# Linear attention into a feed-forward layer: where the block sums of unit 3 and unit 4 stand in the queues

## The chip, the cores and the metric

The kernel runs on one core of a Trainium2 chip. The metric is the device time of one execution in microseconds (us), the median of several runs. Engines are named as in the profile: PE is the matmul engine (TensorE), PEld its weight load, DVE is VectorE, ACT is ScalarE, POOL is GpSimd, and SP (SPq) is the queue from which nearly all DMAs are issued. Each of them takes its instructions strictly in the order in which the program has them, and each waits at an instruction until what that needs is there.

## The reference

For every batch and head a 48 x 48 state is carried along 768 tokens, and the result goes through a feed-forward layer with SiLU.

```
B, H, S, D = 4, 8, 768, 48
for t in range(S):
    kt, vt, rt, wt = k[:, :, t], v[:, :, t], r[:, :, t], w[:, :, t]
    cur = einsum('bhd,bhe->bhde', u * kt, vt)
    y[:, :, t] = einsum('bhd,bhde->bhe', rt, state + cur)
    state = wt[..., None] * state + einsum('bhd,bhe->bhde', kt, vt)
x = y.transpose(0, 2, 1, 3).reshape(B * S, H * D)        # 3072 x 384
h = x @ w_in                                              # 384 x 2048
out = (h * sigmoid(h)) @ w_out                            # 2048 x 384
```

## The kernel before

**Units and passes.** The 768 tokens are cut into 6 chunks of 128, the 4 batches into 2 pairs: 12 units of work (`units`), each with 2 batches and 8 heads. Three stages work on a unit: the attention part (called mix), the first feed-forward matmul with SiLU (`up`, 8 steps), and the second one (`quarter`, 7 steps, a scheme with 7 block products in place of 8; the sums L967 of `sums` prepare its left factors). From unit 3 on, a loop makes one *pass* per unit: pass i holds the attention of unit i, the `up` steps of unit i-1 and the `quarter` steps of unit i-2. The attention of units 0 to 2, and all rounding of the weights, is written out by hand ahead of that loop.

**The order is written by hand.** `mix(i)` returns 13 groups of calls. The loop issues a group, then `ROOM` many of the feed-forward steps, and so on. What is called first stands first in its engine's queue. The scheduler moves nothing; it only adds the semaphore waits.

**A pass of attention.** Group 0 and 1 turn (transpose on DVE, L360) the raw w, k and r of the unit; groups 0 to 2 make running products of w on POOL (`product`, L408) and grow queries and keys by them (L608 on DVE, L626 and L635 on POOL). Levels 3 to 6 are score matmuls on PE (`burst`, L670: levels 3 and 4 together, then 5 and 6), whose outputs are kept in `score` under a mask by DVE (`keep_level`, L680). Levels 5 and 6 use the PSUM rooms p_sc and p_m. `turn_k` (L782, PE) transposes the keys into the two p_m rooms, which level 6 has to leave first. Then `y_state`, `y`, `update` (state: L827 on POOL, L836 on DVE) and `move_x`.

**The blocks of 8 tokens.** Inside a block of 8 tokens the scores aren't matmuls. `block_bonus(i, 0..7)` makes products of r, k, w and u on POOL (L488), `block_sum(i, 0..4)` reduces them on DVE (L522) into `block_sums`, `block_move` sends these through DRAM into another layout, and then `load_rk` fetches the tokens of the next unit. `block_spread` (ACT L549, L551, DVE L552) and `block_write` (DVE L558) put the result into `score`. Step 1 of `block_bonus` multiplies by `u_bc`. Its rows are loaded a second time, in the layout that units from 3 on need, by `load_u` (L259) in unit 2. `make_block_mask` is needed once, in pass 3. From pass 4 on the first products (steps 0 to 3) of unit i+1 are made at the end of pass i, and so are its first two sums and steps 4 and 5, all ahead of the next unit's turns. Pass 3 (`early` is false there, in spite of its name the test is i > 3) makes all steps of its own unit itself.

**Rooms that tie the passes.** `spare` holds three SiLU results of unit 1 until `quarter` of pass 3 has read them, and afterwards the block products (`room_b`), the sums, the moved diagonal and the mask. `quarter` writes into one of two PSUM rooms `p_o`; DVE (L994) or, for the first one, ACT (L992) empties them, so the fourth quarter can't start before DVE has added the second. In DVE's queue that addition stands behind the turns and one L608.

**SP.** The raw loads of unit i+2 (48 small DMAs, L109), the values, `move_x` (L858), the outputs (L998) and the block moves stand in one queue; most issues take about half a microsecond.

Of the kernel before, what the change touches and what calls it, by code (L numbers as in the profile page):

```python
# [8 lines left out]
F32 = mybir.dt.float32  # L9
# [29 lines left out]
def kernel(  # L39
# [11 lines left out]
    nc = tc.nc  # L51
# [4 lines left out]
    NL = 7  # L56
# [12 lines left out]
    NPAIR = 3  # L69
    FIRST = 3  # L70
    BLK = 1 << FIRST


    const = ctx.enter_context(tc.tile_pool(name="const", bufs=1))
# [95 lines left out]
    spare = const.tile([128, NSPARE * 2 * TU], F32, name="spare")  # L170
# [278 lines left out]
    R_AT, K_AT = 0, H * 2 * D  # L449
    room_b = spare[:, 0:768]  # L450
    at = 768
    block_sums = spare[:, at:at + BLK * 2 * BLK]
    at += BLK * 2 * BLK
    block_diag = [spare[:, at + b * H * BLK:at + (b + 1) * H * BLK] for b in range(NB)]
    at += NB * H * BLK
    block_both = spare[:, at:at + NB * H * BLK].rearrange("p (b h s) -> p b h s", b=NB, h=H)
# [11 lines left out]
        return bass.AP(tensor=t.tensor, offset=t.offset + start, ap=[t.ap[0], *dims])  # L468

    def at_sums(start, *dims):  # L470
        t = block_sums
        return bass.AP(tensor=t.tensor, offset=t.offset + start, ap=[t.ap[0], *dims])

    def make_block_mask():

        ids = spare[:, 0:2 * NB].rearrange("p (x b) -> p x b", x=2)
        index = room_b[:, 2 * NB:2 * NB + L].rearrange("p (i s) -> p i s", s=BLK)
        nc.gpsimd.memset(block_sums, 0.0)
        nc.gpsimd.iota(index, pattern=[[BLK, L // BLK], [0, BLK]], base=0, channel_multiplier=0,
                       allow_small_or_imprecise_dtypes=True)  # L480
        nc.vector.tensor_single_scalar(out=ids[:, 0].bitcast(I32), in_=tok_all, scalar=-BLK, op=ALU.bitwise_and)
        nc.vector.tensor_copy(out=ids[:, 1], in_=ids[:, 0].bitcast(I32))
        for b in range(NB):
            nc.vector.tensor_single_scalar(out=block_mask[:, b], in_=index, scalar=ids[:, 1, b:b + 1], op=ALU.is_equal)
# [35 lines left out]
    def block_sum(i, step):  # L520

        add = lambda out, have: nc.vector.tensor_reduce(out=out, in_=have, axis=mybir.AxisListType.X, op=ALU.add)  # L522
        E, S, W = BLK * BLK, BLK, BLK * D
        if step == 0:
            add(at_sums(0, [E, 2], [S + 1, BLK]), ruk[i].rearrange("p (e s d) -> p e s d", e=2, s=BLK))
        elif step == 1:
            add(at_sums(1, [E, 2], [2 * (S + 1), BLK // 2]), room_b[:, 0:W].rearrange("p (e a d) -> p e a d", e=2, d=D))
        elif step == 2:
            for e in range(2):
                for a in range(2):  # L530
                    x = (2 * e + a) * 4 * D
                    add(at_sums(e * E + a * 4 * (S + 1) + 2, [S, 2], [1, 2]),
                        ruk[i][:, x:x + 4 * D].rearrange("p (k q d) -> p k q d", k=2, q=2))
        else:
            e = step - 3
            add(at_sums(e * E + 4, [S, 4], [1, 4]), (room_b, ruk[i])[e].rearrange("p (k q d) -> p k q d", k=4, q=4))
# [325 lines left out]
    def both(fn, i, *args):  # L862
        return [(fn, i, b, *args) for b in range(NB)]

    def block_loads(i):
        return [(load_blocks, i, name, g) for name in "wkr" for g in range(4)]

    def mix(i):

        early = i > NPAIR  # L870
        ahead = i + 1 < len(units)

        def bonus_steps(*steps):
            return [(block_bonus, i, x) for x in steps]

        def sum_steps(*steps):
            return [(block_sum, i, x) for x in steps]

        def pick(first, other):
            return other if early else first  # L880

        next_bonus = [(block_bonus, i + 1, x) for x in range(4)] if ahead else []
        next_sums = [(block_sum, i + 1, 0), (block_sum, i + 1, 1), (block_bonus, i + 1, 4), (block_bonus, i + 1, 5)] if ahead else []
        next_load = [(load_rk, i + 1)] if ahead else []
        placed = [(block_spread, i), (block_write, i)]
        groups = [[*both(turn, i, "w"), (product, i, 0)],
                  [*both(turn, i, "k"), *both(turn, i, "r"), (grow_own, i, 0)],
                  [*[(product, i, l) for l in range(1, NL)], (grow_own, i, 1)],
                  [(odd_keys, i, 2), (grow_keys, i, 2, False), (grow_queries, i, 2), *pick([], sum_steps(2))],
                  [(prepare, i, 3), *pick(bonus_steps(0, 1), bonus_steps(6, 7))],  # L890
                  [(burst, i, 3), (keep_level, i, 3), *pick([(make_block_mask,), *bonus_steps(2, 3), *sum_steps(0)], [*sum_steps(3, 4), (block_move, i), *next_load])],
                  [(keep_level, i, 4), (go_on, i, 4), *pick([*bonus_steps(4), *sum_steps(1)], [])],
                  [(prepare, i, 5), (reverse_v, i), *pick([*bonus_steps(5), *sum_steps(2), *bonus_steps(6, 7)], [])],
                  pick([*sum_steps(3, 4), (block_move, i), *next_load], placed),
                  [(burst, i, 5), (keep_level, i, 5)],
                  [(keep_level, i, 6), (go_on, i, 6), *pick(placed, []), *next_bonus],
                  both(turn_k, i) if i < len(units) - NB else [],
                  [*both(y_state, i), *both(y, i), *both(update, i), *next_sums, (move_x, i)]]

        loads = block_loads(i + NSLOT) if i + NSLOT < len(units) else []  # L900
        if i + 1 < len(units):
            loads.insert(len(loads) // 2, (load_values, i + 1))

        behind = groups[3 if i > NTOK + 1 else 10:]
        for at, group in enumerate(behind):
            group += loads[at * len(loads) // len(behind):(at + 1) * len(loads) // len(behind)]
        return groups
# [104 lines left out]
    def do(*steps):  # L1012
        for fn, *args in steps:
            fn(*args)
# [54 lines left out]
    for m in range(6):  # L1069
# [8 lines left out]
       (bonus, 2, 2), (down, 0, 1, 2), (bonus_sum, 2, 1), (load_rk, 3), (sums, 1, 1), *blocks[3:7], (down, 0, 1, 3))  # L1078
    do((burst, 2, 5), (keep_level, 2, 5), (keep_level, 2, 6), (go_on, 2, 6), (up, 1, 6), (bonus_spread, 2), (bonus_write, 2),
       (load_values, 3), (load_u,), *both(turn_k, 2), (weight_sums, 2), (up, 1, 7), (sums, 1, 2))  # L1080
    do((sums, 1, 3), *both(y_state, 2), *both(y, 2), *both(update, 2), (move_x, 2),
       *blocks[7:])

    ROOM = 1, 1, 1, 2, 2, 1, 1, 1, 2, 1, 1, 1, 0
# [1 line left out]
    for i in range(3, len(units)):  # L1086
        steps = downs(i - 2) + ups(i - 1)
        groups = mix(i)
        if i == NTOK + 1:

            groups[3].insert(0, (weight_sums, 3))
        for group, room in zip(groups, ROOM):
            do(*group)
            for step in steps[:room]:
                do(*step)
            steps = steps[room:]
# [32 lines left out]
```

## Time and profile before

| what | value |
|---|---|
| time | 637.51 us median of 3 (636.78 to 639.26) |
| span of the profiled execution | 635.9 us |
| PE busy | 621.3 us (98%) |
| DVE busy | 441.1 us (69%) |
| POOL busy | 369.0 us (58%) |
| ACT busy | 185.8 us (29%) |
| mean share of DMA engines, HBM traffic | 40.5%, 77 GB/s |
| pass 3, first quarter matmul | 128.0 us |
| pass 4, first quarter matmul | 178.3 us |
| pass 5, first quarter matmul | 237.3 us |
| passes 5 to 9 | 48.75 us each |

The page of a profile gives busy times and 40 equal slices of the span; here a slice is 15.9 us. The other answers of the trace are lists in order of time (start, length in us, engine, line, operation, tiles, and in brackets the idle time ahead of the instruction with what ended it), lists of who waited for whom, and tables by stretch (length, busy time of PE, PEld, DVE, ACT, POOL with the number of instructions, granted PE clock, DMA share, GB/s). The interesting stretch is passes 3 and 4, from 128 to 237 us.

### The profile page before, as it was taken

The numbers are of one execution on the slowest core, as the hardware profiler recorded it, in microseconds if no ns is written. First come the engines' busy times: TensorE is split into PE (matmuls) and PEld (weight loads), VectorE is DVE, ScalarE is ACT, GpSimd is POOL, SyncE is SP. The second block draws the span as 40 slices with busy tenths as digits, with TensorE's granted clock in tenths as the row PEclk, the third lists the DMA queues.
The fourth block names the chain that finished last, engine by engine and source line by source line (L and its number), as shares of the span: only waits on it lengthen the run. The fifth ranks groups of instructions, "written<-read, shape, count | busy, mean of one in ns | idle before, by whom it ended". The sixth has DMA issues, their size and how long they took to land.

```text
span 635.9 us, 12218 instructions
## 1 busy us (share of the span) xinstructions
PE 621.3 (98%) x4574; PEld 563.2 (89%) x4574; DVE 441.1 (69%) x750; ACT 185.8 (29%) x377; POOL 369.0 (58%) x421
## 2 busy tenths in 40 slices
PE   8999999999979999999999999999999999999997
PEld 7888876889868889889889989989989989989997
DVE  7879779885694697588588498588588687561031
ACT  5798881202300320220320320320231221220120
POOL 6998298569478248647557657647747747600000
PEclk9999999999997999999999999999999999999999
DMA  9966954533443643543443453453353222100000
GB/s 225 289 172 141 225 138 50 114 70 65 84 69 54 132 62 53 124 63 51 106 71 53 105 76 53 91 91 53 72 103 52 46 66 51 34 1 26 26 1 25
DMA packets 203291, 53.75 MB, mean 85 GB/s; under 512 B 186464, under 2 KB 194656, under 8 KB 203232
## 3 DMA queue, kind: packets, MB, share of 16 engines
q1 hardware_dynamic: 201648, 52.39, 40.5%
q10 hardware_dynamic: 1584, 0.59, 0.4%
q8 instruction: 36, 0.59, 0.4%
q14 instruction: 23, 0.19, 0.1%
HBM read 43.67 MB, written 5.31 MB: 77 GB/s over the span
## 4 chain that ended last, share of the span: by engine, by line
PE 85%; DVE 4%; POOL 3%; DMA 3%; SPq 2%; issue 1%; ACT 1%; POOLq 0%; DVEq 0%; ACTq 0%
PE p_h L919 36%; PE p_o L985 31%; PE p_sc L670 5%; PE p_m L941 3%; PE p_m L808 3%; PE p_m L795 3%; PE p_m L670 2%; SPq L109 1%; PE p_m L782 1%; POOL tk L626 1%; DMA tokens_w<-in_w_dram 1%; DMA raw<-in_r_dram 1%; DVE temps L967 1%; PE p_sc L822 1%; POOL ruk L488 1%
## 5 line engine op out<-in xcount | busy, mean ns | idle before, releaser
L919 PE MATMUL p_h<-xt,w_in_sb 128*128 128x256 f32 x1152 | 258.1, 382 | 0.7 <-POOL tk L650 0.7
L919 PEld LDWEIGHTS p_h<-xt,w_in_sb 128*128 128x128 f32 x1152 | 215.9, 190 | 32.6 <-POOL tk L650 0.9
L928 ACT ACTIVATE gt<-p_h 128x512 f32<-128x512 f32 x90 | 53.7, 596 | 226.8 <-PE p_h L919 226.7
L626 POOL TENSOR_TENSOR tk<-tk,tw 128x256 f32<-128x256 f32 x126 | 87.8, 718 | 38.1 <-ACT tk L596 18.9
L985 PE MATMUL p_o<-own,temps 128*128 128x192 f32 x528 | 90.7, 333 | 7.0 <-DVE temps L994 7.0
L985 PEld LDWEIGHTS p_o<-own,temps 128*128 128x128 f32 x528 | 88.6, 195 | 7.6 <-DVE temps L994 7.6
L488 POOL TENSOR_TENSOR ruk<-tokens_rk 128x768 f32<-128x768 f32 (+1 forms) x36 | 52.4, 1466 | 69.8 <-DMA tokens_rk<-in_k_dram 36.6
L985 PE MATMUL p_o<-w_out_sb,gt 128*128 128x192 f32 x508 | 87.4, 328 | 0.0
L985 PEld LDWEIGHTS p_o<-w_out_sb,gt 128*128 128x128 f32 x508 | 82.7, 190 | 0.9 <-issue 0.4
L967 DVE TENSOR_TENSOR temps<-gt 128x256 f32<-128x256 f32 x84 | 52.9, 629 | 24.6 <-ACT gt L928 24.6
L608 DVE TENSOR_TENSOR tr<-tr,tw 128x512 f32<-128x512 f32 x62 | 50.7, 818 | 14.7 <-POOL tw L408 11.6
L596 ACT COPY tk<-tk 128x256 f32<-128x256 f32 x51 | 20.5, 402 | 128.8 <-POOL tk L635 104.7
L408 POOL TENSOR_TENSOR tw<-tw 128x256 f32<-128x256 f32 (+6 forms) x83 | 47.8, 576 | 9.2 <-DVE tw L360 5.3
L680 DVE COPY_PREDICATED score<-mask,p_sc 128x512 f32<-128x512 int8 x60 | 42.1, 756 | 11.5 <-PE p_sc L670 10.7
L827 POOL TENSOR_TENSOR state<-state,tw 128x512 f32<-128x512 f32 x16 | 19.4, 1236 | 47.0 <-PE p_m L795 47.0
L670 PEld LDWEIGHTS p_sc<-tr,tk 48*128 48x128 f32 x496 | 30.4, 187 | 10.1 <-issue 6.5
L670 PE MATMUL p_sc<-tr,tk 48*128 48x128 f32 x496 | 36.5, 285 | 0.7 <-POOL tk L626 0.7
L994 DVE TENSOR_TENSOR temps<-p_o,partial 128x192 f32<-128x192 f32 x22 | 7.9, 358 | 35.9 <-PE p_o L985 25.7
L635 POOL TENSOR_TENSOR tk<-tk,tw 128x256 f32<-128x256 f32 x36 | 31.3, 888 | 0.0
L558 DVE COPY_PREDICATED score<-spare 128x1024 f32<-128x1024 int8 x18 | 30.6, 1753 | 0.3
L985 PE MATMUL p_o<-w_out_sb,temps 128*128 128x192 f32 x176 | 30.4, 326 | 0.0
L967 DVE TENSOR_TENSOR temps<-temps,gt 128x256 f32<-128x256 f32 x43 | 29.3, 682 | 1.5
(170 smaller groups left out, 810.8 us busy)
## 6 DMA issues: line engine op xcount, KB each, us to landing
w_out_sb<-in_moe_w_in_dram SPq DMA_DIRECT2D x6, 768.0 KB, 6.8
tokens_rk<-in_r_dram SPq DMA_DIRECT2D x9, 384.0 KB, 4.5
tokens_rk<-in_k_dram SPq DMA_DIRECT2D x9, 384.0 KB, 5.4
tokens_w<-in_w_dram SPq DMA_DIRECT2D x9, 384.0 KB, 6.3
w_out_sb<-in_moe_w_out_dram SPq DMA_DIRECT2D x4, 768.0 KB, 6.2
own<-in_moe_w_out_dram SPq DMA_DIRECT2D x4, 768.0 KB, 4.8
xt<-yt SPq DMA_DIRECT2D x60, 48.0 KB, 2.0
raw<-in_w_dram SPq DMA_DIRECT2D x80, 32.0 KB, 2.9
```

What stands on the lines that cost most here:

```text
L408: engine.tensor_tensor(out=up, in0=t[:, :, 0::2], in1=t[:, :, 1::2], op=ALU.mult)
L488: mul = lambda out, one, two: nc.gpsimd.tensor_tensor(out=out, in0=one, in1=two, op=ALU.mult)
L558: nc.vector.copy_predicated(out=score[:, i % NSC, e].rearrange("p (b q) (i s) -> p b q i s", b=NB, s=BLK), mask=block_mask[:, :, None].to_ ...
L608: nc.vector.tensor_tensor(out=odd, in0=odd, in1=tw[i][l][:, :, 0::2][:, :, :, None].to_broadcast([128, Q, L >> (l + 1), c]), op=ALU.mult)
L626: nc.gpsimd.tensor_tensor(out=out, in0=have, in1=odd_products(i, l, b, *blocks), op=ALU.mult)
L635: nc.gpsimd.tensor_tensor(out=have, in0=have, in1=odd_products(i, l, b, [2, NP * ni]), op=ALU.mult)
L670: nc.tensor.matmul(bass.AP(tensor=s_p.tensor, offset=s_p.offset, ap=[s_p.ap[0], [apart * L // 2, 2], [1, L // 2]]), lhsT=tk[i][rows, X[l % ...
L680: nc.vector.copy_predicated(out=dst, mask=masks[l][:, :, None].to_broadcast([128, NB, NP, ni, c]), data=sc[e].rearrange("p (b q) (i c) -> ...
L919: nc.tensor.matmul(p_h[:, a, :], lhsT=w_in_sb[:, c, f * 128:(f + 1) * 128], rhs=xt[i][:, c, :], start=(c == 0), stop=(c == KC - 1))
L928: nc.scalar.activation(out=gt[i, m], in_=p_h, func=AF.Silu)
L967: nc.vector.tensor_tensor(out=out, in0=one, in1=two, op=op)
L985: nc.tensor.matmul(p, lhsT=left(f), rhs=right[:, f, :], start=(f == 0), stop=(f == FH - 1))
```

## The change

`block_sums` gets a tile of its own instead of a part of `spare`, so that it may be written while `spare` still holds SiLU results, and is zeroed at the start instead of in `make_block_mask`. With that, unit 3's first two products and its first sum are moved to the end of unit 2, ahead of unit 3's turns. In pass 3 the remaining products and sums stand closer together, so that `block_move` and the load of unit 4's tokens are issued earlier, and the spreading and writing of the block scores comes ahead of level 6 (it was behind it). Unit 4 (`late`) has its first two sums behind its turns instead of at the end of pass 3, its products 4 and 5 behind level 3's keys, and its move one group later. Passes from 5 on keep their order. The aim is that unit 4's turns, and with them PE, don't stand behind sums whose products come late.

```diff
-    block_sums = spare[:, at:at + BLK * 2 * BLK]
-    at += BLK * 2 * BLK
+    block_sums = const.tile([128, BLK * 2 * BLK], F32, name="block_sums")
+    nc.gpsimd.memset(block_sums, 0.0)
...
     def make_block_mask():
...
-        nc.gpsimd.memset(block_sums, 0.0)
...
-        next_sums = [(block_sum, i + 1, 0), (block_sum, i + 1, 1), (block_bonus, i + 1, 4), (block_bonus, i + 1, 5)] if ahead else []
+        next_sums = [(block_sum, i + 1, 0), (block_sum, i + 1, 1), (block_bonus, i + 1, 4), (block_bonus, i + 1, 5)] if ahead and early else []
+        late = i == NPAIR + 1
         next_load = [(load_rk, i + 1)] if ahead else []
+        move = [*sum_steps(3, 4), (block_move, i), *next_load]
         placed = [(block_spread, i), (block_write, i)]
...
-                  [*[(product, i, l) for l in range(1, NL)], (grow_own, i, 1)],
-                  [(odd_keys, i, 2), (grow_keys, i, 2, False), (grow_queries, i, 2), *pick([], sum_steps(2))],
-                  [(prepare, i, 3), *pick(bonus_steps(0, 1), bonus_steps(6, 7))],
-                  [(burst, i, 3), (keep_level, i, 3), *pick([(make_block_mask,), *bonus_steps(2, 3), *sum_steps(0)], [*sum_steps(3, 4), (block_move, i), *next_load])],
-                  [(keep_level, i, 4), (go_on, i, 4), *pick([*bonus_steps(4), *sum_steps(1)], [])],
-                  [(prepare, i, 5), (reverse_v, i), *pick([*bonus_steps(5), *sum_steps(2), *bonus_steps(6, 7)], [])],
-                  pick([*sum_steps(3, 4), (block_move, i), *next_load], placed),
-                  [(burst, i, 5), (keep_level, i, 5)],
-                  [(keep_level, i, 6), (go_on, i, 6), *pick(placed, []), *next_bonus],
+                  [*[(product, i, l) for l in range(1, NL)], (grow_own, i, 1), *(sum_steps(0, 1) if late else [])],
+                  [(odd_keys, i, 2), (grow_keys, i, 2, False), (grow_queries, i, 2), *(sum_steps(2) if early and not late else [])],
+                  [(prepare, i, 3), *pick([*bonus_steps(2, 3), *sum_steps(1), *bonus_steps(4, 5)], bonus_steps(4, 5) if late else bonus_steps(6, 7))],
+                  [(burst, i, 3), (keep_level, i, 3), *pick(sum_steps(2), [*sum_steps(2), *bonus_steps(6, 7)] if late else move)],
+                  [(keep_level, i, 4), (go_on, i, 4), *pick([(make_block_mask,), *bonus_steps(6, 7)], move if late else [])],
+                  [(prepare, i, 5), (reverse_v, i), *pick(move, [])],
+                  pick([], placed),
+                  [(burst, i, 5), (keep_level, i, 5), *pick(placed, [])],
+                  [(keep_level, i, 6), (go_on, i, 6), *next_bonus],
...
-    do((sums, 1, 3), *both(y_state, 2), *both(y, 2), *both(update, 2), (move_x, 2),
+    do((sums, 1, 3), *both(y_state, 2), *both(y, 2), *both(update, 2),
+       (block_bonus, 3, 0), (block_bonus, 3, 1), (block_sum, 3, 0), (move_x, 2),
        *blocks[7:])
```

More of the change, by code (lines that the diff above doesn't have):

```diff
@@ L470, in at_sums @@
     def at_sums(start, *dims):
-        t = block_sums
+        t = block_sums[:]
         return bass.AP(tensor=t.tensor, offset=t.offset + start, ap=[t.ap[0], *dims])
```

## The prediction

> **What bounds the kernel now.** I read the page's 40 slices first, then what the matmul engine (PE) waits for, then PE, VectorE (DVE), GpSimd (POOL) and the DMA queue (SPq) in order of time.
>
> ```profile
> PE   8999999999979999999999999999999999999997
> PEclk9999999999997999999999999999999999999999
> ```
>
> PE's longest waits after the start-up (total, times, longest, us):
>
> ```profile
> PE p_o L985 <- DVE temps L994: 7.0, 2, 5.8
> PE p_m L782 <- DVE score L680: 1.2, 1, 1.2
> ```
>
> PE is busy nearly everywhere, so only its gaps can be won, plus the time it runs at a lower clock after one. There is one dent (slice 12, 175 to 191 us), with a dent in the clock behind it. PE's waits past the start-up are 7.0 us for L994 (the DVE addition that empties a p_o bank) and 1.2 us for L680. In order of time, with start, length, and in brackets the idle time:
>
> ```profile
> 137.38 5.47 PE L985 MATMUL p_o<-own,temps 128*128 128x192 f32 x32 [1.28 <-DVE temps L994]
> 192.16 8.05 PE L985 MATMUL p_o<-own,temps 128*128 128x192 f32 x32 [5.76 <-DVE temps L994]
> 229.14 1.24 PE L782 MATMUL p_m<-ident,tk 128*128 128x128 f32 x8 [1.24 <-DVE score L680]
> ```
>
> The second wait opens pass i = 4. Its 32 matmuls also take 8.05 us where the same 32 took 5.47: 2.6 us of slow clock, which the stretches show (PE busy, four other engines, then the granted clock):
>
> ```profile
> 186.40:192.10 5.70, 0.00 (x0) 0.00 (x0) 5.63 (x10) 0.00 (x0) 5.13 (x7) 0.87 0.55 97
> 192.20:197.20 5.00, 5.00 (x16) 5.00 (x17) 3.31 (x7) 0.00 (x0) 4.68 (x8) 0.50 0.22 58
> 197.40:205.30 7.90, 7.90 (x49) 7.71 (x48) 2.41 (x5) 1.33 (x3) 7.30 (x9) 1.00 0.39 51
> ```
>
> So pass 4 loses 5.76 + 2.6 = 8.4 us here. Why is DVE late with L994? It works in order, and ahead of L994 stand the sums L967, the state L836, two block sums L522 and six turns L360:
>
> ```profile
> 174.95 2.04 DVE L967 TENSOR_TENSOR temps<-gt,temps 128x256 f32<-128x256 f32 x1
> 183.63 0.42 DVE L967 TENSOR_TENSOR temps<-temps,gt 128x256 f32<-128x256 f32 x1
> 185.79 0.95 DVE L522 TENSOR_REDUCE spare<-ruk 128x16 f32<-128x768 f32 x1
> 187.12 1.29 DVE L360 STREAM_TRANSPOSE tw<-raw 128x512 f32<-128x512 f32 x2
> 191.74 0.36 DVE L994 TENSOR_TENSOR temps<-p_o,partial 128x192 f32<-128x192 f32 x1
> ```
>
> An L967 takes 0.42 us alone, and 1.1 to 2.0 us from 174.95 to 183.6, while POOL multiplies without a break (174.63 to 183.3). POOL is there because pass 4's tokens came late: their load stands on SPq behind block_move, which waited for the last block sum (165.7).
>
> **What the Trainium skill says.** "SBUF — State Buffer" (SBUF: two separate sides) has GpSimd and two-input VectorE operations exclude each other from a shared port pair; the trace agrees (0.42 against 1.1 to 2.0 us). "TensorE: Matmul & The Clock Gate" (What's actually happening) gives the half clock after an idle window of about 3.4 us, and the full one after about as long busy; the trace has 0.50 after 5.76 us idle, for some 5 us. "DMA: Bandwidth & Descriptors" (Two DMAs through the same engine are not ordered) says that only a completion semaphore shows that data landed, so a reader waits for the landing, not for the issue; here the smallest landings take 1.8 us (4 KB, diag) and 1.9 (16 KB, raw).
>
> **The change, part by part.** No PE instruction moves, and nothing is added but order; the zeroing of block_sums (0.22 us on POOL) goes to the start-up, beside POOL's wait of 1.9 us there: nothing. Three moves matter.
>
> *1. Pass 3's first block products and first sum go to the end of pass 2.* They are queued ahead of the turns: on POOL two products behind the state update, on DVE one reduction between L836 and L360. The second product multiplies by u_bc, whose new layout is loaded by load_u.
>
> ```profile
> 131.23 1.12 DVE L836 TENSOR_TENSOR state<-p_sc,state 48x384 f32<-48x384 f32 x2
> 132.36 1.30 DVE L360 STREAM_TRANSPOSE tw<-raw 128x512 f32<-128x512 f32 x2
> 136.97 0.36 DVE L994 TENSOR_TENSOR temps<-p_o,partial 128x192 f32<-128x192 f32 x1
> 135.75 1.38 SPq L259 DMA_DIRECT2D u_bc<-in_u_dram x2
> 148.06 1.82 POOL L488 TENSOR_TENSOR ruk<-ruk,u_bc 128x768 f32<-128x768 f32 x1
> ```
>
> Before, u_bc was read at 148.06, long after it landed. Now the reader is ready at about 131 (POOL's state update ends at 128.43, and one product takes 1.8 to 2.1 us), and u_bc isn't there: SPq issues one DMA after another from 119.6 on, and its order up to here is the same in the changed program. The trace has no reader to time this landing. Taking 1.9 us (1.8 to 3.0 as bounds, vt's 192 KB being the 3.0) from the second issue at 136.5 gives 138.4; product 1.82, to 140.2; reduction 0.95, to 141.2. The turns, which stood at 132.36, start 8.8 us later (8.7 to 9.9). Behind them on DVE is L994 at 136.97, for which PE already waits 1.28 us with both p_o banks full; nothing hides the shift. PE restarts at 146.2 instead of 137.38: **+8.8**. It has then been idle 10 us, so the half clock comes as in pass 4: **+2.6** (0 if the window falls luckily; 2.6 is the only measured value). POOL's products of the same unit shift by 8.8 too, under the 11.4 of PE, so the level-3 scores (147.98) don't wait on top.
>
> *2. The rest of unit 3's products run together behind level 3, and the write of the blocks is put ahead of level 6.* By hand: POOL's keys of level 3 end at 146.2 + 8.8 = 155; the products at 6.3 us (the L488 rows from 151.48 to 161.09 without gaps) to 161.4; level 4 1.2; mask and DVE's reading of it to 165.7; two products at 1.8, to 169.4; the last sum, 170.4. Block_move goes then, 7 us earlier against PE (165.77 + 11.4 = 177.2), and frees the tokens: 8.9 us from move to POOL's first product in pass 3, so 179.3. Level 5's burst on PE is at 163.11 + 11.4 = 174.5; DVE keeps it to 176.9, writes the blocks (0.2 + 2.5) to 179.6, and then has four L967 ahead of level 6's keep, now just when POOL begins 6.2 us of products. At pass 4's rates:
>
> ```profile
> 222.90 1.22 DVE L967 TENSOR_TENSOR temps<-gt 128x256 f32<-128x256 f32 x1
> 224.15 1.92 DVE L967 TENSOR_TENSOR temps<-temps,gt 128x256 f32<-128x256 f32 x1
> 225.99 1.21 DVE L967 TENSOR_TENSOR temps<-gt 128x256 f32<-128x256 f32 x1
> 227.13 1.23 DVE L967 TENSOR_TENSOR temps<-gt,temps 128x256 f32<-128x256 f32 x1
> ```
>
> that is 5.4 us, to 185.0; the first keep, 0.65, frees a p_m bank at 185.7. PE's turn_k (L782, 170.38 + 11.4 = 181.8) waits for it: **+3.8**. If the tokens land after the sums it is 0, since four L967 alone take 1.4.
>
> *3. Unit 4's first sums go behind its turns; its later products, move and write are shifted inside pass 4.* Its first products on POOL are over by 186, so the remaining sums run near 0.42 us, and 1.4 us of L522 leaves the turns' path. Passes 5 to 9 keep two L522 there and start every 48.75 us without a gap at L994, so pass 4 should too: **-8.4**. Pass 4's keys aren't delayed: bonus steps 4 and 5 (4.3 us) end before its level 3 burst needs POOL again. Its own wait of 1.24 stays, since move and tokens keep their distance to level 5 (the last sum comes at about 219.2, was 212.67 + 6.7 = 219.4).
>
> Sum: 8.8 + 2.6 + 3.8 - 8.4 = +6.8 us, **644 us**.
>
> **The rivals.**
> - *The wait is there, but level 6 isn't hit*: 8.8 + 2.6 - 8.4 = +3.0, and without pass 4's 1.24, +1.8: about 640. For it: the overlap hangs on one microsecond of tokens. Against: POOL's products last 6.2 us, a wide target.
> - *More is lost*: u_bc lands at 139.5, or pass 4 keeps half of its wait: +10 to +13, about 649. For it: queues shift by 11 us and DMAs may meet. Against: passes 5 to 9 heal themselves.
> - *Faster*: u_bc lands by 131, as if the order on SPq cost nothing. Then the first move costs a reduction (0.95) and some 1.6 of sums slowed by POOL; with the 3.8 and the -8.4 that is -2, without the 3.8 -5.9: about 633. Against it: the issue at 135.75 is measured, and SPq before it has no gap to close.
>
> **How the numbers follow.** Forecast 0.55, milder 0.22, worse 0.10, faster 0.13. 638 to 648 holds the first two and the lower edge of the third. Slower than 640.7: the forecast, the worse and a third of the milder, 0.73. Within 0.5%: most of the milder and a little of the faster, 0.16. Faster than 634.3: 0.11.
>
> **What would show it.** Step 1: POOL idle 5 to 8 us ahead of ruk<-ruk,u_bc near 138, a DVE wait for POOL as long at the new L522, and PE's first wait for L994 near 10 us with a clock of 0.50 behind it. Step 2: PE waiting 3 to 4 us at L782 in pass 3, with L967 at 1.2 us or more. Step 3: no wait for L994 in pass 4. The forecast falls if POOL runs that product at about 131, or if PE's first wait is under 4 us.

## The result, and the profile after

| | before | after |
|---|---|---|
| time, median | 637.6 us | 646.9 us |
| spread of 4 runs | 636.78 to 639.26 | 646.59 to 648.59 |
| span of the profiled execution | 635.9 us | 644.8 us |
| mean granted PE clock | 0.995 | 0.986 |
| PE waits past the start-up | 8.2 us | 15.9 us |
| passes 3 and 4, first quarter matmul of pass 3 to that of pass 5 | 109.3 us | 118.7 us |

The changed kernel is slower: ratio 1.0148, interval [1.0121, 1.0175]. The forecast was 644 us with a range of 638 to 648. The lines have moved by up to one: in the profile after, L994 of before is L995, L985 is L986, L782 is L781, L680 is L679, L967 is L968, L522 is L521, L488 is L487. In e4, f3 and g1 below only the lines from L919 on have moved.

The 40 slices of PE and of its clock: there are two dents now, a deep one in slice 9 (129 to 145 us) and one in slice 12 (177 to 193 us), where the only one of before stood; but it is a new one, as the waits show.

```profile
PE   8999999949979999999999999999999999999998
PEclk9999999987989999999999999999999999999999
```

What PE waited for (total, times, longest, us). The wait for L995 is one wait now, not two; that for L679 is new in pass 3.

```profile
PE p_o L986 <- DVE temps L995: 10.9, 1, 10.9
PE p_m L781 <- DVE score L679: 5.0, 2, 3.9
```

PE in order of time, pass 3 and the start of pass 4:

```profile
146.46 8.34 PE L986 MATMUL p_o<-own,temps 128*128 128x192 f32 x32 [10.86 <-DVE temps L995]
186.36 1.86 PE L781 MATMUL p_m<-ident,tk 128*128 128x128 f32 x8 [3.86 <-DVE score L679]
188.01 3.68 PE L920 MATMUL p_h<-xt,w_in_sb 128*128 128x256 f32 x12
201.31 7.96 PE L986 MATMUL p_o<-own,temps 128*128 128x192 f32 x48
```

The reader is to see four things. Pass 3 opens with a wait of 10.86 us, and the 32 matmuls behind it take 8.34 us instead of 5.47. PE then waits 3.86 us at the transposed keys. Behind that wait too the matmuls are slow: 1.86 us for 8 that took 1.04 in pass 3 of before, 3.68 for 12 that took 2.76. And pass 4 (201.31) has no bracket: its 5.76 us are gone, as intended.

Who made pass 3 wait stands in the rows of POOL and DVE:

```profile
138.76 1.80 POOL L487 TENSOR_TENSOR ruk<-ruk,u_bc 128x768 f32<-128x768 f32 x1 [8.88 <-DMA u_bc<-in_u_dram]
140.59 0.95 DVE L521 TENSOR_REDUCE block_sums<-ruk 128x16 f32<-128x768 f32 x1 [7.26 <-POOL ruk L487]
141.47 1.29 DVE L360 STREAM_TRANSPOSE tw<-raw 128x512 f32<-128x512 f32 x2
146.05 0.36 DVE L995 TENSOR_TENSOR temps<-p_o,partial 128x192 f32<-128x192 f32 x1
```

POOL was idle 8.88 us for `u_bc`, DVE 7.26 us for POOL, the turns stand at 141.47 instead of 132.36, and L995 at 146.05 instead of 136.97: one chain, shifted whole. And in pass 3's end, the sums ahead of level 6's keep:

```profile
180.14 0.41 DVE L968 TENSOR_TENSOR temps<-gt 128x256 f32<-128x256 f32 x1
180.58 1.92 DVE L968 TENSOR_TENSOR temps<-temps,gt 128x256 f32<-128x256 f32 x1
182.42 2.02 DVE L968 TENSOR_TENSOR temps<-gt 128x256 f32<-128x256 f32 x1
184.36 1.21 DVE L968 TENSOR_TENSOR temps<-gt,temps 128x256 f32<-128x256 f32 x1
185.50 1.33 DVE L679 COPY_PREDICATED score<-mask,p_m 128x512 f32<-128x512 int8 x2
```

The first of the four takes 0.41 us. Then POOL's products of unit 4 begin (180.38), and the other three take 1.2 to 2.0 us. L679, the last line, is the keep that PE waits for.

The balance from the start of pass 3 to that of pass 5, against before:

| term | forecast, us | measured, us | how |
|---|---|---|---|
| wait for L995 in pass 3 | +8.8 | +9.58 | 10.86 - 1.28 |
| slow clock behind it | +2.6 | +2.87 | 8.34 - 5.47 |
| wait for level 6's keep, pass 3 | +3.8 | +3.86 | 3.86 - 0 |
| slow clock behind that | not in the sum | +1.74 | (1.86 - 1.04) + (3.68 - 2.76) |
| pass 4's wait and its slow clock | -8.4 | -8.34 | 5.76 + (8.05 - 5.47) |
| pass 4's wait at the keys | 0 | -0.14 | 1.10 - 1.24 |
| sum | +6.8 | +9.57 | the stretch itself grew by 9.43 |

### The profile page after: what moved, and what is told of

Its sections match the earlier page's. It is cut to its first block, busy times and chain, and to the rows that moved or that the text cites. A ratio compares the mean times of both kernels' runs of the same rounds, so it can differ in the third digit from the quotient of the medians.

```text
span 644.8 us, 12217 instructions
## 1 busy us (share of the span) xinstructions
PE 622.8 (97%) x4574; PEld 564.6 (88%) x4574; DVE 441.3 (68%) x750; ACT 185.9 (29%) x377; POOL 367.1 (57%) x421
## 4 chain that ended last, share of the span: by engine, by line
PE 90%; DVE 4%; POOL 1%; ACT 1%; SPq 1%; issue 1%; DMA 0%; POOLq 0%; ACTq 0%
PE p_h L920 38%; PE p_o L986 31%; PE p_sc L669 5%; PE p_m L942 3%; PE p_m L807 3%; PE p_m L794 3%; PE p_m L669 2%; DVE temps L968 2%; PE p_m L781 1%; PE p_sc L821 1%; POOL tk L625 1%; PE p_m L1021 1%; DVE score L679 1%; PE p_m L372 1%; PE p_m L845 0%
## 5 line engine op out<-in xcount | busy, mean ns | idle before, releaser
L920 PE MATMUL p_h<-xt,w_in_sb 128*128 128x256 f32 x1152 | 259.0, 382 | 0.7 <-POOL tk L649 0.7
L920 PEld LDWEIGHTS p_h<-xt,w_in_sb 128*128 128x128 f32 x1152 | 216.7, 191 | 32.9 <-POOL tk L649 0.9
L929 ACT ACTIVATE gt<-p_h 128x512 f32<-128x512 f32 x90 | 53.7, 596 | 233.2 <-PE p_h L920 233.1
L625 POOL TENSOR_TENSOR tk<-tk,tw 128x256 f32<-128x256 f32 x126 | 86.3, 706 | 33.4 <-ACT tk L595 14.6
L986 PE MATMUL p_o<-own,temps 128*128 128x192 f32 x528 | 90.7, 333 | 10.9 <-DVE temps L995 10.9
L986 PEld LDWEIGHTS p_o<-own,temps 128*128 128x128 f32 x528 | 88.9, 195 | 11.2 <-DVE temps L995 11.2
L487 POOL TENSOR_TENSOR ruk<-tokens_rk 128x768 f32<-128x768 f32 (+1 forms) x36 | 52.2, 1461 | 67.6 <-DMA tokens_rk<-in_k_dram 35.9
L986 PE MATMUL p_o<-w_out_sb,gt 128*128 128x192 f32 x508 | 87.4, 328 | 0.0
L986 PEld LDWEIGHTS p_o<-w_out_sb,gt 128*128 128x128 f32 x508 | 82.7, 190 | 0.9 <-issue 0.4
L968 DVE TENSOR_TENSOR temps<-gt 128x256 f32<-128x256 f32 x84 | 51.8, 617 | 26.7 <-ACT gt L929 26.7
L607 DVE TENSOR_TENSOR tr<-tr,tw 128x512 f32<-128x512 f32 x62 | 51.1, 824 | 13.1 <-POOL tw L408 10.0
L679 DVE COPY_PREDICATED score<-mask,p_sc 128x512 f32<-128x512 int8 x60 | 42.1, 755 | 16.2 <-PE p_sc L669 15.3
L968 DVE TENSOR_TENSOR temps<-temps,gt 128x256 f32<-128x256 f32 x43 | 32.3, 752 | 1.5
L521 DVE TENSOR_REDUCE block_sums<-ruk 128x4 f32<-128x192 f32 (+1 forms) x54 | 27.2, 544 | 8.3 <-POOL ruk L487 8.1
L995 DVE TENSOR_TENSOR temps<-p_o,partial 128x192 f32<-128x192 f32 x22 | 7.9, 357 | 35.9 <-PE p_o L986 25.7
L634 POOL TENSOR_TENSOR tk<-tk,tw 128x256 f32<-128x256 f32 x36 | 31.3, 888 | 0.0
L557 DVE COPY_PREDICATED score<-spare 128x1024 f32<-128x1024 int8 x18 | 30.6, 1751 | 0.3
```

Source lines behind the costliest of these rows:

```text
L487: mul = lambda out, one, two: nc.gpsimd.tensor_tensor(out=out, in0=one, in1=two, op=ALU.mult)
L557: nc.vector.copy_predicated(out=score[:, i % NSC, e].rearrange("p (b q) (i s) -> p b q i s", b=NB, s=BLK), mask=block_mask[:, :, None].to_ ...
L607: nc.vector.tensor_tensor(out=odd, in0=odd, in1=tw[i][l][:, :, 0::2][:, :, :, None].to_broadcast([128, Q, L >> (l + 1), c]), op=ALU.mult)
L625: nc.gpsimd.tensor_tensor(out=out, in0=have, in1=odd_products(i, l, b, *blocks), op=ALU.mult)
L634: nc.gpsimd.tensor_tensor(out=have, in0=have, in1=odd_products(i, l, b, [2, NP * ni]), op=ALU.mult)
L679: nc.vector.copy_predicated(out=dst, mask=masks[l][:, :, None].to_broadcast([128, NB, NP, ni, c]), data=sc[e].rearrange("p (b q) (i c) -> ...
```

## The experiments

My theory was that of the forecast: the first move makes DVE stand behind the landing of `u_bc` (call it W), and the earlier tokens let POOL's products fall on the sums ahead of level 6. The rival was that the place of the first move costs as much with `u_bc` on hand, and that something else keeps the gain of unit 4's part from being had. All ratios are to the kernel before, timed on the same chip.

### W: the landing of u_bc, brought forward and put back

**e1_load_u_early.** The kernel after, with `load_u` behind `load_rk(3)`:

```diff
-       (bonus, 2, 2), (down, 0, 1, 2), (bonus_sum, 2, 1), (load_rk, 3), (sums, 1, 1), *blocks[3:7], (down, 0, 1, 3))
+       (bonus, 2, 2), (down, 0, 1, 2), (bonus_sum, 2, 1), (load_rk, 3), (load_u,), (sums, 1, 1), *blocks[3:7], (down, 0, 1, 3))
...
-       (load_values, 3), (load_u,), *both(turn_k, 2), (weight_sums, 2), (up, 1, 7), (sums, 1, 2))
+       (load_values, 3), *both(turn_k, 2), (weight_sums, 2), (up, 1, 7), (sums, 1, 2))
```

> The changed kernel with load_u issued right behind load_rk(3) (near 121 us instead of 135.8), nothing else. Theory W (unit 3's turns wait for the landing of u_bc through product and sum): POOL's second product starts at 130 without idle, the sum at about 133; what stays of the first move is 2 to 2.5 us (one reduction, and sums slowed by POOL), so PE's wait at the third quarter group falls from 10.9 to about 3.7 us and its slow clock (2.9 us) goes or shrinks: 637 to 640 us. Rival P (the place of product and sum ahead of the turns costs by itself, by the port shared with POOL): PE's wait stays above 8 us, 645 us or more. Rival L (the write ahead of level 6 is the loss): no change, 647.

Measured: 643.23 us, 1.0088 [1.0070, 1.0107]. PE's wait falls from 10.86 to 5.23 us, not to the 1.3 of before. W is thus 5.6 us of it; the other 4.0 belong to the place. POOL and DVE of this kernel, in order of time, say what they are:

```profile
128.41 1.98 POOL L487 TENSOR_TENSOR ruk<-tokens_rk 128x768 f32<-128x768 f32 x1
130.48 1.87 POOL L487 TENSOR_TENSOR ruk<-ruk,u_bc 128x768 f32<-128x768 f32 x1
```

```profile
128.77 1.91 DVE L968 TENSOR_TENSOR temps<-temps,gt 128x256 f32<-128x256 f32 x1
130.60 2.03 DVE L968 TENSOR_TENSOR temps<-gt 128x256 f32<-128x256 f32 x1
135.48 0.95 DVE L521 TENSOR_REDUCE block_sums<-ruk 128x16 f32<-128x768 f32 x1
```

POOL has no bracket: nothing waits for `u_bc` any more. But two products of 1.9 us fall on two of the eight sums at the end of pass 2, which take 1.91 and 2.03 us instead of 0.42 (the next one, behind the products, takes 0.41 again): 3.1 us, and the reduction is 0.95. The expectation of 637 to 640 us was 3.2 us too low at its upper end: PE's wait was to be 3.7 us, the 5.23 us of idle still bring the slow clock (7.99 us for the 32), and the wait at the keys grew to 4.66, with 2.9 us of slow clock behind. The rivals, at 645 us and more, fell too.

**e5_load_u_later.** The kernel after, with `load_u` put behind `move_x(2)`, and the two products and the sum behind that:

```diff
-       (block_bonus, 3, 0), (block_bonus, 3, 1), (block_sum, 3, 0), (move_x, 2),
+       (move_x, 2), (load_u,), (block_bonus, 3, 0), (block_bonus, 3, 1), (block_sum, 3, 0),
```

> The changed kernel with load_u issued behind the ten DMAs of move_x(2), so 6.4 us later (their time on the queue). Theory W: every microsecond is paid, POOL's product at about 145, PE's wait at about 17 us, 653 us. Rivals P and L: no change, 647.

Measured: 653.81 us, 1.0261 [1.0245, 1.0276], as expected. The wait is passed on one to one: POOL's product comes 6.67 us later than in the kernel after (145.43 against 138.76), PE's wait is 6.62 us longer (17.48).

```profile
145.43 1.80 POOL L487 TENSOR_TENSOR ruk<-ruk,u_bc 128x768 f32<-128x768 f32 x1 [15.51 <-DMA u_bc<-in_u_dram]
```

**f4_first_move_undone.** The kernel after, with unit 3's first two products and its first sum back in pass 3:

```diff
-                  [(prepare, i, 3), *pick([*bonus_steps(2, 3), *sum_steps(1), *bonus_steps(4, 5)], bonus_steps(4, 5) if late else bonus_steps(6, 7))],
+                  [(prepare, i, 3), *pick([*bonus_steps(0, 1), *sum_steps(0), *bonus_steps(2, 3), *sum_steps(1), *bonus_steps(4, 5)], bonus_steps(4, 5) if late else bonus_steps(6, 7))],
...
-       (block_bonus, 3, 0), (block_bonus, 3, 1), (block_sum, 3, 0), (move_x, 2),
+       (move_x, 2),
```

> The changed kernel with the first move alone undone: products 0 and 1 and the first sum of unit 3 in pass 3 again, in the group of level 3's keys; all else as changed. Theory W: PE's wait at the third quarter group is 1.3 us again and its slow clock goes, 12.4 us less; but block_move then comes about 7 us later against PE, so the write, now ahead of level 6, makes PE wait 5 us or so at turn_k: 637 to 641. If the first move isn't the loss: 645 or more.

Measured: 637.96 us, 1.0012 [0.9999, 1.0025], as expected; PE waits 1.44 us for L995 in pass 3, and 5.68 us at the keys, with 2.1 us of slow clock behind. So the whole loss against before goes with the first move, and the rest of the change pays at the keys of pass 3 what it saves in pass 4 (5.68 + 2.1 against 8.34).

### The wait at level 6

**e2_write_behind.** The kernel after, with pass 3's write back behind level 6:

```diff
-                  [(burst, i, 5), (keep_level, i, 5), *pick(placed, [])],
-                  [(keep_level, i, 6), (go_on, i, 6), *next_bonus],
+                  [(burst, i, 5), (keep_level, i, 5)],
+                  [(keep_level, i, 6), (go_on, i, 6), *pick(placed, []), *next_bonus],
```

> The changed kernel with pass 3's spreading and writing of the blocks put back behind level 6, nothing else. Theory W: the wait of 10.9 us stays; only PE's wait of 3.9 us at L781 in pass 3 goes, with the slow clock behind it (1.7 us), since the four sums then run from 177.5, ahead of POOL's products at 180.4: 641 to 642 us. Rival L: all of the loss goes, 638 or less. Rival P: 641 as well.

Measured: 646.54 us, 1.0161 [1.0127, 1.0196]: the wait in pass 3 is gone, and nothing is won, where 641 to 642 us were expected. It comes back in pass 4, 1.58 us for L995 and 3.71 at the keys (1.10 in the kernel after). The 1.58 come from the write: it now runs beside POOL's products and takes 4.65 us instead of 2.49, and three of the sums behind it take 1.2 us each. Pass 4's last block sum ends at 217.8 us (216.84 + 0.94), and its move could go then, but SP is at its raw loads:

```profile
218.28 1.96 SPq L109 DMA_DIRECT2D raw<-in_w_dram  x4
220.35 0.38 SPq L540 DMA_DIRECT2D kept<-block_sums  x1
```

DVE waits 7.0 us for the moved blocks in pass 4 and comes late to level 6. This I had not foreseen: the time of this move is set by SP's queue, not by the sums.

**f1_keep6_first.** The kernel after, with level 6 kept right behind level 5 in every pass from 3 on, ahead of write and sums:

```diff
-                  [(burst, i, 5), (keep_level, i, 5), *pick(placed, [])],
-                  [(keep_level, i, 6), (go_on, i, 6), *next_bonus],
+                  [(burst, i, 5), (keep_level, i, 5), (keep_level, i, 6), *pick(placed, [])],
+                  [(go_on, i, 6), *next_bonus],
```

> The changed kernel with level 6 kept right behind level 5 in every pass from 3 on, ahead of the write of the blocks and of the four sums; nothing else. Theory S (what stands between the two keeps on DVE, the block write and four sums slowed by POOL's port, holds the p_m rooms from PE): the waits at turn_k go (3.9 in pass 3, 1.1 in pass 4) with the slow clock of pass 3 (1.7), and the 10.9 us stay: about 640.2. Rival Q (what PE gains in pass 3 is given back in pass 4, since the DMA queue there can't send block_move any earlier): 645 to 647, with a new wait in pass 4.

Measured: 643.3 us, 1.0087 [1.0063, 1.0112]. Both waits at the keys are gone, which shows that what stood between the two keeps, write and sums, made them. e2 tells the two apart: there the four sums still stood ahead of the keep but ran before POOL's products, at 0.40 to 0.42 us each, and the wait in pass 3 was gone as well. So it takes the write, which puts the sums off until POOL multiplies, and the sums slowed by that. The time misses the 640.2 us expected by 3.1, since a smaller wait takes their place, with 1.7 us of slow clock: `y_state` waits for L607, which now stands behind write and slowed sums.

```profile
188.22 3.63 PE L794 MATMUL p_m<-tr,state 128*128 128x128 f32 x16 [2.42 <-DVE tr L607]
```

**f2_early_keep6.** The edits of e1 and f1 together.

> The changed kernel with load_u right behind load_rk(3) and level 6 kept right behind level 5. If theory W (u_bc) and theory S add up: 643.2 less 5.9 us of waits at turn_k and 2.9 us of slow clock behind them, 634 to 635; PE's wait at the third quarter group stays at 5.2, made of the reduction and of sums slowed by POOL's two products. Rival Q: 640 or more.

Measured: 637.45 us, 1.0004 [0.9992, 1.0015], where 634 to 635 were expected. The waits are those of e1 (5.24) and f1 (2.42), each with its slow clock; the second was not in the expectation. With the wait for `u_bc` and those at the keys gone, the change is still worth nothing. Against before, the place of the first products costs 5.24 - 1.28 us and 1.77 of slow clock, the wait at `y_state` 2.42 and 1.48, together 9.6; the change saves 8.34 in pass 4's opening and 1.24 at its keys, 9.6 too.

### Unit 4's part, and what bars its gain

One thing must be set right first: in the kernel before, pass 3 already makes the first products and sums of the next unit, unit 4, at its end; POOL's products from 174.63 us on are these.

**e4_unit4_alone.** The kernel before, with unit 4's part of the change only; its core:

```diff
-        next_sums = [(block_sum, i + 1, 0), (block_sum, i + 1, 1), (block_bonus, i + 1, 4), (block_bonus, i + 1, 5)] if ahead else []
+        next_sums = [(block_sum, i + 1, 0), (block_sum, i + 1, 1), (block_bonus, i + 1, 4), (block_bonus, i + 1, 5)] if ahead and early else []
+        late = i == NPAIR + 1
...
+                  [*[(product, i, l) for l in range(1, NL)], (grow_own, i, 1), *(sum_steps(0, 1) if late else [])],
...
+                  [(keep_level, i, 4), (go_on, i, 4), *pick([*bonus_steps(4), *sum_steps(1)], [*sum_steps(3, 4), (block_move, i), *next_load] if late else [])],
```

> The kernel before with unit 4's part alone: its first two sums behind its turns, products 4 and 5 behind level 3's keys, move one group later; pass 3 and block_sums as before. If the two sums on the turns' path are what made pass 4 late: the wait of 5.8 us in pass 4 goes, 629 to 630 us. If it is the sums L967 slowed by POOL's late products (theory W's reading): only the 1.4 us of two reductions go, PE waits 4.4 us, its slow clock stays: 636 us.

Measured: 641.48 us, 1.0061 [1.0043, 1.0079], slower, which neither expectation had (629 to 630, or 636). The wait for L995 falls to 4.60 only, with the slow clock unchanged (7.95 us for the 32), and the wait at pass 4's keys grows from 1.24 to 3.83, since the move goes at 214.24 with the sums done at 211.4. The profile is that of the fastest run, 639.99 us; why the other three took 641.4 to 641.9 stays open. Taking 1.4 us of reductions out of the turns' path is not the cure for 5.76 us.

**f3_before_mended.** e4, with keep 6 first, and unit 4's first products put behind pass 3's state update:

```diff
-                  [*both(y_state, i), *both(y, i), *both(update, i), *next_sums, (move_x, i)]]
+                  [*both(y_state, i), *both(y, i), *both(update, i), *([] if early else next_bonus), *next_sums, (move_x, i)]]
```

> The kernel before, with unit 4's part of the change alone, level 6 kept right behind level 5, and the first four products of unit 4 moved behind the state update of pass 3. If the sums of pass 3 are late only because POOL's products hold the port: the wait of 5.8 us in pass 4 goes with its slow clock (2.6), and so do the waits at turn_k: 629 to 630. If pass 4 is late for want of tokens or raw loads: 635 to 638.

Measured: 636.19 us, 0.9979 [0.9972, 0.9986]. The waits at the keys are gone, the one for L995 is still 4.81 us. The products went behind the state update, to 177.55 to 183.8, where the twelve sums were still running (174.6 to 185.5): L968 takes 2.03 us at 177.79 and 1.92 at 179.86. The number falls in the expectation's second branch (want of tokens or raw loads), but the rows show the first cause still at work, so this run can't tell the two apart. To move the products by three microseconds was not enough; h1 takes them off the sums.

**h1_own_products and h2_own_raw_spread.** h1 is the kernel before, with no product made a pass ahead: passes 4 to 11 are ordered as its pass 3 is. The sums go the same way as the products (`next_sums` is empty too). The last two lines of the diff are in h2 only, which issues pass 3's raw loads earlier, where SP is idle ahead of pass 3's block move.

```diff
         def pick(first, other):
-            return other if early else first
+            return first
...
-        next_bonus = [(block_bonus, i + 1, x) for x in range(4)] if ahead else []
+        next_bonus = [(block_bonus, i + 1, x) for x in range(4)] if False else []
...
-                  [(burst, i, 3), (keep_level, i, 3), *pick([(make_block_mask,), *bonus_steps(2, 3), *sum_steps(0)], [*sum_steps(3, 4), (block_move, i), *next_load])],
+                  [(burst, i, 3), (keep_level, i, 3), *pick([*([] if early else [(make_block_mask,)]), *bonus_steps(2, 3), *sum_steps(0)], [*sum_steps(3, 4), (block_move, i), *next_load])],
...
-        behind = groups[3 if i > NTOK + 1 else 10:]
+        behind = groups[3 if i > NTOK + 1 else 5:]
```

> The kernel before, with every pass from 4 on ordered like its pass 3: all products and sums of a unit in its own pass, none at the end of the pass ahead. Theory (what costs pass 4 its 5.76 us at L994 is only that POOL's products run beside DVE's sums): no wait for L994 in pass 4, clock 1.0 there, and the 1.24 at L782 gone, 637.2 - 5.8 - 2.6 - 1.2 = 627.6 us, 626 to 630. Rival (SPq has no gap from 170 us on, so a block move that is put later leaves later than in pass 3): a wait of 3 to 5 us with slow clock at L782 or L795 of pass 4 and of later passes, 633 to 645.

> As h1, and pass 3's raw loads spread from group 5 on in place of group 10, so that SPq issues them in its idle time ahead of pass 3's block move. Theory: nothing is left for it to win, as h1 within 1 us, 626 to 630. Rival (SPq full): 3 to 6 us faster than h1.

Measured: h1 634.56 us, 0.9955 [0.9940, 0.9970]; h2 627.53 us, 0.9850 [0.9834, 0.9867]. Theory and rival each had a part. h1 fell into the rival's range. h2 is where the theory had put both, but 7.0 us faster than h1, where the rival said 3 to 6 and the theory nothing. In h1 there is no wait for L994 in pass 4 and no slow clock, as the theory said; and there is a new wait of 5.2 us at L795, as the rival said. DVE, SP and PE of h1:

```profile
210.12 0.95 DVE L522 TENSOR_REDUCE spare<-ruk 128x16 f32<-128x768 f32 x1 [0.82 <-POOL ruk L488]
```

```profile
215.92 5.13 SPq L109 DMA_DIRECT2D raw<-in_k_dram  x8
221.15 0.40 SPq L541 DMA_DIRECT2D kept<-spare  x1
```

```profile
227.65 3.42 PE L795 MATMUL p_m<-tr,state 128*128 128x128 f32 x16 [5.24 <-ACT kq L783]
```

The sums are done at 211.1 us and the move goes at 221.15: SP issues without a gap from 167 us on and is 10 us behind. ACT, which spreads the moved blocks before it copies the keys, waits 8.05 us for them, and PE for ACT. In h2 the sums are done at 211.1 us again, and the queue is 1.2 us behind instead of 10 (SP, then the 40 slices of PE):

```profile
208.31 3.90 SPq L109 DMA_DIRECT2D raw<-in_k_dram  x8
212.30 0.40 SPq L541 DMA_DIRECT2D kept<-spare  x1
```

```profile
PE   8999999999999999999999999999999999999997
```

PE has no dent left, and its clock is 1.000 on average.

**g1_unit4_in_pass4.** As h2 for unit 4 alone, with keep 6 first; units 5 to 11 have their first products made a pass ahead, as before:

```diff
+        next_bonus = [(block_bonus, i + 1, x) for x in range(4)] if ahead and early else []
+        late = i == NPAIR + 1
...
+                  [(prepare, i, 3), *pick(bonus_steps(0, 1), bonus_steps(0, 1, 2, 3) if late else bonus_steps(6, 7))],
+                  [(burst, i, 3), (keep_level, i, 3), *pick([(make_block_mask,), *bonus_steps(2, 3), *sum_steps(0)], [*sum_steps(0, 1), *bonus_steps(4, 5), *sum_steps(2), *bonus_steps(6, 7)] if late else [*sum_steps(3, 4), (block_move, i), *next_load])],
+                  [(keep_level, i, 4), (go_on, i, 4), *pick([*bonus_steps(4), *sum_steps(1)], [*sum_steps(3, 4), (block_move, i), *next_load] if late else [])],
...
+                  [(burst, i, 5), (keep_level, i, 5), (keep_level, i, 6)],
+                  [(go_on, i, 6), *placed, *next_bonus],
```

> The kernel before, with unit 4's products and sums all in pass 4, level 6 kept ahead of the write, and pass 3's raw loads from group 5 on; from unit 5 on the first products are made in the pass ahead, as in the kernel before. Theory: the block move of pass 4 and the load of unit 5's tokens behind it come some 5 us later than in the kernel before, so unit 5's products now run beside the sums at the end of pass 4: the wait for L994 leaves pass 4 and comes back in pass 5, 637.2 - 8.4 - 1.2 + 4 to 8 = 632 to 636 us. Rival: it doesn't come back, 627 to 630.

Measured: 634.73 us, 0.9956 [0.9941, 0.9971], as expected: pass 4's wait for L995 is 0.18 us, and pass 5 now has one of 2.54, with POOL's products (219.25 to 225.3) on the sums at the end of pass 4. A further 1.95 us goes at L920, and 1.7 us of slow clock behind it (these 12 matmuls take 2.76 us elsewhere, and the 16 of L670 that follow 1.51 instead of 1.16):

```profile
212.01 4.13 PE L920 MATMUL p_h<-xt,w_in_sb 128*128 128x256 f32 x12 [1.95 <-ACT gt L929]
```

The queues say why. ACT waits 5.02 us at L596 for POOL's keys (L626) ahead of that L929, and POOL has unit 4's products, up to 209.3 us, ahead of the keys. In both places where the switch to working a pass ahead was tried, between passes 3 and 4 and between 4 and 5, the late tokens made a wait.

**i1_raw_spread_alone.** The kernel before, with the last edit of h2 alone:

```diff
-        behind = groups[3 if i > NTOK + 1 else 10:]
+        behind = groups[3 if i > NTOK + 1 else 5:]
```

> The kernel before with one edit: pass 3's raw loads from group 5 on in place of group 10; products and sums stay where the kernel before has them. Theory (two separate causes: products beside the sums make the wait of 5.76 us for L994 with its 2.6 us of slow clock, and SPq's full queue only bars a later block move): the 5.76 stays, the 1.24 at L782 may go, 636 to 637.5 us. Rival (SPq alone is the cause, and products could have stayed): 628 to 630.

Measured: 635.76 us, 0.9973 [0.9964, 0.9983], as expected within 0.3 us. The wait at the keys of pass 4 is gone, the one for L994 stays:

```profile
192.09 7.63 PE L985 MATMUL p_o<-own,temps 128*128 128x192 f32 x32 [5.85 <-DVE temps L994]
```

So the four kernels before, i1, h1 and h2 form a square, two edits each done or not. The raw loads alone give 1.6 us, the products alone 2.9, and both 10.0: the waits that the products make hide most of what the full queue costs. The 10.0 agree with what before loses there: 5.76 + 2.58 in pass 4's opening and 1.24 at its keys, 9.6 us.

## Why the prediction was right, point by point

- **Step 1, the wait for u_bc.** Right. Estimated landing 138.4 us; the product, which waited for it, starts at 138.76. Turns at 141.2 estimated, 141.47 measured; PE back at 146.2 estimated, 146.46 measured. The estimate of 1.9 us from issue to landing was some 0.3 short, as the second issue starts at 136.6 in the kernel after. PE is back 9.08 us later than before; the wait grew by 9.58 because PE came to it 0.5 us earlier. POOL's idle time of 8.88 us lies outside the 5 to 8 named as a sign, since POOL was ready at 129.9 and not at 131. e5 shows that the landing passes to PE one to one; e1 shows that it is 5.6 us of the extra wait, and that 4.0 would be there without it. The rival "faster" put that place at 2.55 us (a reduction and some 1.6 us of slowed sums), 1.4 short.
- **Its slow clock.** Right, 2.87 us for 2.6, but the size is in part luck: behind waits as long, 10.51 us in e2 and 10.84 in f1, the same 32 matmuls took 7.27 and 6.85 us, so the slow clock cost 1.8 and 1.4. The Trainium skill's "TensorE: Matmul & The Clock Gate" (What's actually happening) names an idle window of about 3.4 us as what halves the clock; 10.86 us are well past it, and the first 5 us behind it ran at 0.50. The stretch of the kernel after (length, busy time of PE, PEld, DVE, ACT, POOL, then the granted clock):

```profile
146.50:151.50 5.00, 5.00 (x16) 5.00 (x17) 3.17 (x4) 0.00 (x0) 4.62 (x7) 0.50 0.40 49
```

- **Step 2, the products on the sums ahead of level 6.** Right in time and mechanism: tokens estimated at 179.3, products at 180.38; keep estimated to free the bank at 185.7, PE back at 186.36; +3.8 estimated, +3.86 measured. The four sums took the 5.4 us estimated, though not one by one: the first escaped POOL (0.41), the third took 2.02 instead of 1.21. f1 and e2 show the cause: the wait is gone when the keep comes ahead of write and sums, and when the sums run ahead of POOL's products.
- **The term that was mis-sized.** To the +3.8 of step 2 no slow clock was added, and no reason was given for that. It measured +1.74 us: the idle time of 3.86 us was followed by a slow clock as that of 5.76 was. This is 1.74 of the 2.8 us by which the sum fell short; 0.78 is PE's longer first wait and 0.27 that wait's clock. So 646.9 us lies nearer to the rival "more is lost" (649) than to the 644 of the forecast; that it is the forecast which held is told by the waits, not by the time.
- **Step 3, pass 4.** Right: no wait for L995, -8.34 for -8.4, and 1.10 us left at the keys where 1.24 were to stay. Of the two reasons given, e4 shows the sizes: the 1.4 us of reductions alone leave 4.60 of the 5.76 us; the greater share is that POOL is done with unit 4's first products at 186.4 us, ahead of the last twelve sums (187.32 on, the first eight at 0.42 us each). h1 shows that with neither products nor reductions there the wait is gone altogether. In the kernel after that in turn needs the tokens early. The two moves hang together: the earlier tokens that free pass 4 are those that hit level 6 in pass 3.
- **The rivals.** "Milder" fell, since level 6 was hit. Of the two causes of "more is lost" (649) neither came: `u_bc` was there by 138.76, and pass 4 kept nothing of its wait. "Faster" fell on the landing; its issue at 135.75 us stands in before. e1 gave that rival its premise, `u_bc` in time, and it fell again: 6.1 us slower than before, not faster, as the place cost 1.4 us more than it had said and brought the slow clock, and the wait at the keys grew.

What stays open: how PE's clock decides on short idle times (below), and e4's slower runs.

## What to carry to other kernels

When an instruction is moved ahead, look up when each of its inputs is *issued and landed*, not only when the old reader ran: here an input that was ready at least 9 us early (`u_bc`, by 138.76 us for a reader at 148.06) became the last to come, and everything in order behind it was shifted. When work is moved off a collision, ask where it lands: a sum that fell on POOL's products took two and a half to five times its length (1.1 to 2.0 us for 0.42), and every version here that only shifted the products paid in the next place. And before an early result is counted as a gain, check that the queue which has to send it is free at that time; issuing raw loads earlier, 16 of them in an idle stretch of that queue (155 to 163 us in h2), turned a gain of 2.9 us into one of 10.0.

## What the runs showed of the hardware

- Short idle times sometimes cost clock, and sometimes not. In f1, 2.42 us of idle were followed by 3.63 us for the 16 matmuls of L794 that take 1.95 (granted clock 0.52); in f2 the same wait by 3.43 (0.54). In g1, 2.54 us of idle cost nothing: 32 matmuls of L986 took 5.47. But an idle time of 1.95 us in the same run, at L920, cost 1.7: the clock was still 1.00 for the first microsecond behind it (212 to 213 us), and 0.50 from 214 to 216. All 17 waits of 3.71 us and more in these runs were followed by a slow clock, which cost 1.4 to 2.9 us. So a wait of two to two and a half us is to be counted with 0 to 1.7 us on top. The window of about 3.4 us named above is no safe limit here: the measurement decides, and it says that 2 us can be enough.
- A sum that began just ahead of a product kept its 0.42 us (174.61 in the kernel before), and the product, begun at 174.63, took 2.07 us instead of 1.8; the sums that came later in the product took 1.1 to 2.0.
- COPY_PREDICATED with both sources in SBUF slows beside POOL as the additions do: f1's write (L557, two of them) took 4.12 us while POOL multiplied, 2.49 in the kernel after without POOL. The keep L679, whose source is in PSUM, didn't slow: two took 1.33 us beside POOL (185.50 in the kernel after) and 1.33 without (176.26). The transposes L360 don't slow: two of them took 1.29 us at 187.12 in the kernel before, beside POOL, and 1.29 at 141.47 in the kernel after, with POOL idle.
- A small issue on SP takes about half a microsecond (16 raw loads in 7.97 us in h2, ten of `xt` in 6.25). So the queue can be full while the DMA engines aren't: in h1 from 170 to 220 us SP had no gap, and the engines were busy 46%.
